# One more attention head keeps its scores in PSUM, and nine thread priorities of a planned emission order move by small steps

## The chip, the cores and the metric

The kernel runs on one core of a Trainium2 chip. The metric is device time in microseconds of one execution, lower is better; the median of several executions is compared. The engines are named as in the profile: PE (TensorE matmuls), PEld (its weight loads), DVE (VectorE), ACT (ScalarE), POOL (GpSimd), and SP, whose queue issues most of the DMAs.

## The reference, cut to what matters

Three layers run in a row, for 4 batches of 576 tokens, 512 wide.

```python
# 1: attention, 8 heads of 64, with a decay per key and a causal mask
scores = scale * q @ k.T + (cum[:, None] - cum[None, :]); scores[causal] = -1e9
attn = softmax(scores); x = concat_heads(attn @ v)
# 2: four attention experts, the best two of four by a gate, causal
for e in range(4):
    q, k, v = x @ wq[e], x @ wk[e], x @ wv[e]
    y += gate[:, e] * (softmax(scale * q @ k.T + mask) @ v @ wo[e])
# 3: low-rank mixing over tokens, then a feed-forward layer of width 2048
u = y + (y.T @ U @ V).T
out = u + relu(u @ w_ch1) @ w_ch2
```

The weights of the third layer come as float64 and are converted in the kernel; products that need it are made as three f16 products of high and low parts.

## The kernel before, in words

Work is written as some hundred Python generators, the threads. A thread yields the name of an engine when it wants to emit instructions on it, or an event, or a buffer ring. The class `Plan` holds a clock of its own for every engine and picks, again and again, the thread with the smallest key. The key is the planned start time in ns plus `PEN` (35.0) times the thread's priority from the table `PR`. So a step of 1 in `PR` is worth 35 ns of planned time; threads whose engine is busy have the same planned start, and then the smaller priority goes first whatever the distance. The order in which steps are picked is the order of the instructions in every engine's queue, and each engine runs its queue in that order.

```python
k = (k + PEN * th["prio"], th["prio"], th["seq"], k)
if best is None or k < best[0]:
    best = (k, th)
```

The heads are taken in the order of `HEADS`, written (layer, batch, head): the eight heads of batch 0 in layer 1, then (1,1,0) and (1,1,1), the four experts (2,0,0) to (2,0,3), the other six heads of batch 1, then experts and heads of the following batches by turns. Counted from 0, (1,1,0) is head 8 and (1,1,1) head 9.

`scores` (L514) makes each head's scores in five row blocks, 64, 192, 320, 448 and 576 keys wide, into PSUM: a ring `sp` of three banks, the widest block in two halves. `softmax` (L542) finds the row minimum of the negated scores with the mask added on DVE, and takes the exponential on ACT into the SBUF tile `sc`. A head counted below `EARLY` does this differently from the others: DVE writes the masked scores back into the same PSUM bank, ACT reads that bank, and the bank is handed back after the exponential; its widest block takes the double bank `acc` (which the feed-forward output uses later) and no `sp` bank. For all other heads DVE writes into `sc`, which has to be free by then, and the `sp` bank is handed back right after DVE.

The exponentials go to `P` as a high part (ACT or DVE) and a low part (mostly POOL). SP then turns them by transposing DMAs into `pt` and `PT`, or, for the first six heads and some experts, PE turns them through its identity matmul (L625). `pair_pv` multiplies by the values, `pv_out` scales into `xn`, splits into `xh` and turns it by DMA into `xt`. `project` (L808) makes queries and keys of layer 2 from `xt`; in batches 1 to 3 it makes its first half, waits for `values_gates` (L845: values and gates, five blocks), and then makes its second half. Both use the two `mm` banks. `prep` (L1045) loads and converts the float64 weights; `fold` (L1014) multiplies the converted tiles `x` by `wtr` into the bank `hid`. `hidden` and `outputs` (L1207, L1240) are the feed-forward layer, in 10 groups of 256 tokens, which PE can take up whenever a group's input `z` is there.

Of the kernel before, what the change touches and what calls it, by code (L numbers as in the profile page):

```python
# [31 lines left out]
XHB = 2  # L32
PBUFS = (1, 1, 1)
VGAT = (2, 1)
EARLY = 8
QUEUE = ('act', 'act', 'sp', 'act')
ACTDMA = 500
PEN = 35.0
# [2 lines left out]
LAG = 800.0  # L41
AHEAD = 5
PROJ_EXP = 15
PR = {'load': 0.5, 'low0': 1.75, 'low': -4, 'zeros': -4, 'scores': 2, 'soft0': 0.75, 'soft2_0': 0.5, 'soft': 3, 'soft2_': 4.75, 'pv0': 2, 'pv': 2, 'pvout0': -4, 'pvout': 3, 'project0': 5, 'project': -4, 'vg0': -1, 'vg': 1.5, 'out0': -2.25, 'out': 9, 'values0': 1.25, 'values': 3, 'wall': 1.75, 'prep': 5, 'f64': -0.25, 'f64_2': 1.25, 'fold': 1.25, 'wf': 2.75, 'w2': 2.5, 'mix': -3.75, 'relu': 2.25, 'store': 0, 'hidden': 4.25, 'outputs': 4.75}
TERMS = ((0, 0), (0, 1), (1, 0))

TURN = {(1, 0): 3, (2, 0): 2, (1, 1): 0, (1, 3): 0}
# [110 lines left out]
class Plan:  # L158
# [21 lines left out]
    def spawn(self, gen, prio=1, t=None):  # L180
        self.seq += 1
        th = {"gen": gen, "t": self.now() if t is None else t, "prio": prio, "seq": self.seq, "last": None}
        self.threads.append(th)
        self.step(th, None)
# [58 lines left out]
def attn_moe_mixer(ctx: ExitStack, tc: tile.TileContext, qk, v, f, wall, wot, wo, w1, w2, u3, v3, out):  # L243
# [208 lines left out]
    def ev(*name):  # L452
        if name not in E_:
            E_[name] = Event(plan)
        return E_[name]
# [58 lines left out]
    def scores():  # L514
        yield ev("mask")
        for key in HEADS:
            yield ev("loaded", key)
            whole, early = key[0] == 1, key in HEADS[:EARLY]

            ops = [(x[:, 0], x.rearrange("d t s -> d (t s)")) for x in HG[key]]  # L520
            for blk in range(KB):
# [4 lines left out]
                for c0, c1 in ([(0, n)] if n <= 512 else [(0, 288), (288, 576)]):  # L526
# [8 lines left out]
                    st.append((sp, c0, c1))  # L535
                spawn(softmax(key, blk, st, early, both), PR[('soft2_' if key[0] == 2 else 'soft') + ('0' if key[1] == 0 else '')])
            if not whole:
# [4 lines left out]
    def softmax(key, blk, st, early, both):  # L542
# [7 lines left out]
        if blk == 0 and on_pe:  # L550
            spawn(turn_head(key), PR['soft0'])
        if first and blk < 2 and not on_pe:
# [56 lines left out]
    def turn_head(key):  # L609

        pt = yield r_pt
        PT[key, True] = pt
        n = Event(plan, 5)
        yield ev("identr")
        for c, blks, k0, k1 in ((0, (0, 1), 0, 5), (3, (2,), 0, 5), (6, (3,), 0, 5), (10, (4,), 0, 4), (14, (4,), 4, 5)):
            for blk in blks:
                yield ev("exp", key, blk)
            r, bank = yield Either(*((r_mm, r_hid) if key[1] == 0 else (r_mm,)))
            flat = bank.rearrange("q a k -> q (a k)") if r is r_hid else bank
            i = 0  # L620
            for blk in blks:
                x = EXP[key, blk]
                yield "pe"
                for kb in range(k0, min(k1, blk + 1)):
                    nc.tensor.transpose(flat[:, 128 * i:128 * i + 128], x[:, 128 * kb:128 * kb + 128], identr)  # L625
                    plan.tensor(110, 128)
                    i += 1
                if k1 > blk:
                    r_sc[blk].free(EXP.pop((key, blk)))

            def out_(r=r, bank=bank, flat=flat, c=c, i=i):
                hi, lo = (pt[:, 15 * t + c:15 * t + c + i, :].rearrange("k c q -> k (c q)") for t in range(2))
                yield from split(hi, lo, flat[:, :128 * i], 2.0 ** 14)
                r.free(bank)
                n.done()
            spawn(out_(), PR['soft0'])
        yield n
        ev("turned", key, 1).done()
# [24 lines left out]
    def pair_pv(kind, b, p):  # L663
# [12 lines left out]
        for j in range(2):  # L676
# [25 lines left out]
            r_pt.free(pt)  # L702
            spawn(pv_out(kind, b, p, j, bank, pv), PR['pvout0' if b == 0 else 'pvout'])
        if not on_pe:
# [7 lines left out]
    def pv_out(kind, b, p, j, bank, pv):  # L712

        h = 2 * p + j
        if kind == 1:
            x = XH[b, p]
        else:
            x = natural(b)[:, p]
        rr = yield r_rr
        yield "dve"  # L720
        if kind == 1:
            ts(rr, pv[:, :, 64], EPS, ALU.add, RV[b][p // 2], ALU.mult)
        else:
            ts(rr, pv[:, :, 64], EPS, ALU.add)
        recip(rr, rr)
        if kind == 2:
            yield ev("gate", b)
            yield "dve"
            tt(rr, rr, GATE[b][:, :, h], ALU.mult)
            if count(E, "gated", b).n == 1:  # L730
                r_wq.free(GATE[b])
            count(E, "gated", b).done()
        xn = yield r_xn
        yield "dve"
        tt(xn, pv[:, :, 0:64], rr[:, :, None].to_broadcast([128, KB, 64]), ALU.mult)
        r_mm.free(bank)
        r_rr.free(rr)
        hi, lo = (x[:, i, :, 64 * j:64 * j + 64] for i in range(2))
        yield from parts(hi, lo, xn)
        r_xn.free(xn)  # L740
        both = count(2, "split", kind, b, p)
        both.done()
        if j == 0:
            return
        yield both
        if p == 0:
            if kind == 1:
                XT[b] = yield r_xt
            else:
                YT[b] = yield r_ynz.of([128, 2, 2, 640], F16, "yt")  # L750
            ev("turn", kind, b).done()
        yield ev("turn", kind, b)
        yield "sp"
        to = (XT if kind == 1 else YT)[b][:, p].rearrange("d t (c q) -> d (t c) q", q=128)
        done = dma(to, x.rearrange("q t c d -> q (t c d)"), transpose=True)
        if kind == 1:
            r_xh.free(x, done.t)
        count(4 if kind == 1 else 2, "out", kind, b).done(done.t)
# [6 lines left out]
    def values(b):  # L765

        es, ss, last = [], [], []
        for half in range(2):
            mx = col(f"mxv{b}{half}", 2)
            vrs = []  # L770
            for i in range(2):
                vr = yield r_vr
                if half == 1 and b == 0:
                    yield ev("rows of first")
                yield QUEUE[3]
                hp = 2 * half + i
                got = dma(vr, v[b][:, :, hp * 128:(hp + 1) * 128], queue(3))
                vrs.append((vr, got))
            for i, (vr, got) in enumerate(vrs):
                yield got  # L780
                junk = yield r_xn.of([128, KB, 128], F16, "junk")
                yield "act"
                abssum(mx[:, i:i + 1], vr, junk)
                r_xn.free(junk)
            e = yield from pow2(f"v{b}{half}", mx, 2)
            es.append(e)
            ss.append(scales(f"v{b}{half}", e, 14)[0])
            if half == 1:
                yield "dve"
                e = col(f"ev{b}")  # L790
                ts(e, es[0], es[1], ALU.max)
                SV[b] = scales(f"v{b}", e, 14)
                RV[b] = [times(f"rv{b}{i}", s, SV[b][1]) for i, s in enumerate(ss)]
                ev("sv", b).done()
            for i, (vr, got) in enumerate(vrs):
                hp = 2 * half + i
                hi = yield r_vp[0]
                lo = yield r_vp[1]
                VP[b, hp] = (hi, lo)
                x = vr.rearrange("p k (h d) -> p k h d", h=2)  # L800
                yield from split(hi[:, :, :, 0:64], lo[:, :, :, 0:64], x, ss[half])
                r_vr.free(vr)
                ev("vp", b, hp).done()
        if b + 1 < B:
            spawn(values(b + 1), PR['values'])


    def project(b):  # L808
# [8 lines left out]
        for p in range(2):  # L817
# [4 lines left out]
            for t in (1, 0):  # L822
                hi, lo = (stg[:, 1], stg[:, 0]) if t else (stg[:, 2], stg[:, 3])
                for c in range(2):
# [8 lines left out]
                    def out_(hi=hi[:, cs], lo=lo[:, cs], pp=pp, n=n):  # L833
                        yield from split(hi, lo, pp[:, :288], float(2.0 ** -PROJ_EXP))
                        r_mm.free(pp)
                        n.done()
                    spawn(out_(), PR['out0' if b == 0 else 'out'])
            ev("project", b, p).done()
# [631 lines left out]
```

## Time and profile before

| | us |
|---|---|
| median of 3 runs (lowest to highest) | 731.06 (730.34 to 732.14) |
| profiled execution, device time | 730.98 |
| its span, first to last instruction | 729.3 |
| PE busy / PEld busy | 652.0 / 450.4 |
| DVE busy / ACT busy / POOL busy | 441.2 / 404.0 / 223.2 |

In the rows further down a line of a timeline reads: start and duration in us, engine, source line (a helper's line, so most have L261, L266, L272 or L284), operation, output<-input, shapes, count, and in square brackets the time that the engine was idle just before it and what ended that. A DMA row of SP gives the time that the issue held the queue. PEclk is the granted share of TensorE's full clock.

### The profile page before, as it was taken

To read this page: it belongs to the slowest core of one execution; us is meant where nothing else is said; L and a number is where in the kernel's file an instruction comes from. 1 tells how busy PE (TensorE), PEld (TensorE's weight loads), DVE (VectorE), ACT (ScalarE), POOL (GpSimd) and SP (SyncE) were. 2 spreads that over 40 slices of the span, in tenths; PEclk is the share of its full clock that TensorE was granted. 3 is DMA by queue.
4 is the path that set the end of the run, shared out by engine and by line. 5 is a ranking of instruction groups with operands and counts; after the bars stand their busy time and mean duration, and the time that the engine had idled before them with its cause. 6 is when DMAs were issued, how large, how long until landed. Compare 5 with 4: busy or idle time off the path is not lost. (4 is left out here: it accounts for less than half of the span.)

```text
span 729.3 us, 15198 instructions
## 1 busy us (share of the span) xinstructions
PE 652.0 (89%) x5622; PEld 450.4 (62%) x5622; DVE 441.2 (60%) x1532; ACT 404.0 (55%) x844; POOL 223.2 (31%) x292
## 2 busy tenths in 40 slices
PE   3777969877678999999998999999999899999997
PEld 2555757756455677577665776676667556665653
DVE  6999887899888746465754376667524653211111
ACT  4757776677778735577765374678623652212121
POOL 4021441101387501355654033465520350000000
PEclk9989999999889999999999999999999999999999
DMA  7735799586567633899877268898842881000000
GB/s 214 197 89 131 168 227 280 148 218 209 122 130 142 96 84 83 173 171 173 158 164 129 64 142 164 142 175 156 160 92 55 140 154 28 30 1 30 1 30 29
DMA packets 206351, 92.94 MB, mean 127 GB/s; under 512 B 178884, under 2 KB 190404, under 8 KB 206244
## 3 DMA queue, kind: packets, MB, share of 16 engines
q1 hardware_dynamic: 195636, 86.59, 55.7%
q10 hardware_dynamic: 10640, 5.38, 2.9%
q8 instruction: 44, 0.72, 0.4%
q14 instruction: 31, 0.25, 0.1%
HBM read 35.68 MB, written 5.16 MB: 56 GB/s over the span
## 5 line engine op out<-in xcount | busy, mean ns | idle before, releaser
L284 POOL TENSOR_TENSOR P<-sc,P 128x192 f16<-128x192 f32 (+4 forms) x186 | 149.3, 816 | 217.2 <-ACT P L266 185.4
L261 PE MATMUL acc<-w2x,g 128*128 128x512 f16 x768 | 180.6, 379 | 2.5 <-DVE nm L272 0.8
L261 PEld LDWEIGHTS <-g 128*128 128x128 f16 x864 | 83.3, 98 | 88.4 <-DVE g L272 2.7
L266 ACT ACTIVATE sc<-sc,nm 128x576 f32<-128x576 f32 (+4 forms) x200 | 108.4, 555 | 37.4 <-DVE nm L272 34.6
L272 DVE SCALAR_TENSOR_TENSOR g<-hid,g 128x512 f16<-128x512 f32 x72 | 49.6, 689 | 119.1 <-ACT g L266 118.9
L261 PE MATMUL hid<-z,wfr 128*128 128x256 f16 x864 | 109.4, 274 | 5.7 <-DVE g L272 2.8
L261 PE MATMUL sp<-Y 128*128 128x192 f32 (+4 forms) x352 | 105.3, 421 | 9.5 <-DVE nm L272 8.3
L266 ACT ACTIVATE g<-hid 128x512 f16<-128x512 f32 x72 | 42.5, 590 | 108.7 <-PE acc L261 47.0
L261 PEld LDWEIGHTS <-wfr 128*128 128x128 f16 x864 | 83.5, 98 | 26.9 <-issue 7.5
L266 ACT ACTIVATE P<-sc 128x576 f16<-128x576 f32 (+4 forms) x183 | 79.9, 460 | 27.4 <-DMA pt<-P 25.0
L261 PEld LDWEIGHTS sp<-Y 128*128 128x128 f32 x352 | 62.0, 202 | 30.2 <-DVE nm L272 15.8
L261 PE MATMUL mm<-V,pt 128*128 128x65 f16 x2046 | 74.0, 194 | 6.3 <-DMA pt<-P 3.8
L261 PEld LDWEIGHTS <-pt 128*128 128x128 f16 x2046 | 69.1, 98 | 10.4 <-DMA pt<-P 4.6
L272 DVE CUSTOM_DVE_ANT_0 sc<-sp,mask 128x192 f32<-128x192 f32 (+4 forms) x120 | 50.8, 426 | 7.3 <-PE sp L261 4.0
L261 PE MATMUL mm<-xt,wall 128*128 128x288 f16 x384 | 50.8, 286 | 3.7 <-DVE stg L272 2.1
L261 PEld LDWEIGHTS <-wall 128*128 128x128 f16 x384 | 37.0, 98 | 16.4 <-issue 4.0
L272 DVE CUSTOM_DVE_ANT_0 sc<-sp,mask,cols 128x288 f32<-128x288 f32 (+4 forms) x80 | 38.6, 489 | 11.1 <-PE sp L261 8.1
L284 POOL TENSOR_TENSOR xh<-xn,xh 128x320 f16<-128x320 f32 x29 | 24.6, 849 | 60.9 <-ACT xh L266 46.0
L261 PE MATMUL hid<-x,wtr 128*128 128x256 f32 x128 | 33.0, 399 | 5.4 <-DVE nm L272 4.4
L284 POOL TENSOR_TENSOR y<-xn,y 128x320 f16<-128x320 f32 x16 | 13.2, 826 | 66.1 <-ACT y L266 61.4
L261 PE MATMUL sp<-Xh 128*128 128x64 f16 (+2 forms) x192 | 29.8, 277 | 1.8 <-DVE nm L272 1.2
L261 PEld LDWEIGHTS hid<-x,wtr 128*128 128x128 f32 x128 | 24.1, 200 | 9.8 <-DVE nm L272 4.3
(142 smaller groups left out, 866.0 us busy)
## 6 DMA issues: line engine op xcount, KB each, us to landing
wd<-in_w SPq DMA_DIRECT2D x32, 512.0 KB
Y<-in_qk SPq DMA_DIRECT2D x32, 288.0 KB
vr<-in_v ACTq DMA_DIRECT2D x16, 320.0 KB
out_dram<-o SPq DMA_DIRECT2D x17, 256.0 KB
Xh<-stg SPq DMA_DIRECT2D x16, 216.0 KB
Xh<-stg SPq DMA_DIRECT2D x16, 144.0 KB
w2x<-in_wall SPq DMA_DIRECT2D x4, 386.0 KB
pt<-P SPq DMA_TRANSPOSE x76
```

What stands on the lines that cost most here:

```text
L261: nc.tensor.matmul(out_, lhsT=lhsT, rhs=rhs, start=start, stop=stop, **kw)
L266: nc.scalar.activation(out_, in_, fn, **kw)
L272: getattr(nc.vector, op)(**kw)
L284: getattr(nc.gpsimd, op)(out=out_, **kw)
```

## The change: what it does

`EARLY` goes from 8 to 9, so head 8 is handled like the eight before it. In `PR` eleven values move. Two of them, `low0` and `low`, are read by no line of the kernel. The nine others: `zeros` (memsets at the start) -4 to -2.5, `pv0` and `pv` 2 to 2.5, `project0` 5 to 6.75, `vg` (values and gates of batches 1 to 3) 1.5 to 3.25, `values0` 1.25 to 1, `wall` 1.75 to 1.5, `prep` 5 to 4.75, `w2` 2.5 to 2.75. No instruction is added or removed apart from head 8's other operands.

```diff
-EARLY = 8
+EARLY = 9
...
-PR = {'load': 0.5, 'low0': 1.75, 'low': -4, 'zeros': -4, 'scores': 2, 'soft0': 0.75, 'soft2_0': 0.5, 'soft': 3, 'soft2_': 4.75, 'pv0': 2, 'pv': 2, 'pvout0': -4, 'pvout': 3, 'project0': 5, 'project': -4, 'vg0': -1, 'vg': 1.5, 'out0': -2.25, 'out': 9, 'values0': 1.25, 'values': 3, 'wall': 1.75, 'prep': 5, 'f64': -0.25, 'f64_2': 1.25, 'fold': 1.25, 'wf': 2.75, 'w2': 2.5, 'mix': -3.75, 'relu': 2.25, 'store': 0, 'hidden': 4.25, 'outputs': 4.75}
+PR = {'load': 0.5, 'low0': 2, 'low': -1.75, 'zeros': -2.5, 'scores': 2, 'soft0': 0.75, 'soft2_0': 0.5, 'soft': 3, 'soft2_': 4.75, 'pv0': 2.5, 'pv': 2.5, 'pvout0': -4, 'pvout': 3, 'project0': 6.75, 'project': -4, 'vg0': -1, 'vg': 3.25, 'out0': -2.25, 'out': 9, 'values0': 1, 'values': 3, 'wall': 1.5, 'prep': 4.75, 'f64': -0.25, 'f64_2': 1.25, 'fold': 1.25, 'wf': 2.75, 'w2': 2.75, 'mix': -3.75, 'relu': 2.25, 'store': 0, 'hidden': 4.25, 'outputs': 4.75}
```

## Rows read from the trace of the kernel before

**Rows 1.** Busy time by stage: us, busy us (instructions) per engine, granted clock, DMA.

```profile
0.00:110.00 110.00, 77.40 (x649) 58.77 (x650) 93.59 (x299) 73.71 (x154) 32.87 (x67) 0.96 0.70 171
110.00:207.00 97.00, 78.50 (x717) 60.15 (x717) 82.69 (x258) 68.37 (x149) 19.18 (x21) 0.94 0.74 192
207.00:225.00 18.00, 13.78 (x109) 9.59 (x109) 17.13 (x55) 14.16 (x28) 14.84 (x14) 0.91 0.52 88
225.00:588.00 363.00, 345.72 (x3237) 240.30 (x3236) 214.91 (x852) 216.27 (x461) 147.22 (x182) 1.00 0.70 136
588.00:729.00 141.00, 136.59 (x919) 81.64 (x915) 32.85 (x70) 31.53 (x56) 9.07 (x11) 1.00 0.14 33
```

**Rows 2.** PE in order of time: head 9's scores to the projection, first feed-forward matmul.

```profile
97.12 0.59 PE L261 MATMUL sp<-Y 128*128 128x192 f32 x2 [1.64 <-DVE nm L272]
97.83 1.99 PE L261 MATMUL hid<-x,wtr 128*128 128x256 f32 x8
99.66 2.42 PE L261 MATMUL sp<-Y 128*128 128x320 f32 x8
102.02 1.45 PE L261 MATMUL mm<-V,pt 128*128 128x65 f16 x42
107.83 3.49 PE L261 MATMUL hid<-x,wtr 128*128 128x256 f32 x8 [4.06 <-DVE nm L272]
111.16 3.10 PE L261 MATMUL mm<-xt,wall 128*128 128x288 f16 x24
...
206.28 0.27 PE L261 MATMUL hid<-z,wfr 128*128 128x256 f16 x1
```

**Rows 3.** DVE in order of time: head 7's 448 block, head 8's, the converted tile.

```profile
81.73 0.63 DVE L272 CUSTOM_DVE_ANT_0 sp<-sp,mask 128x448 f32<-128x448 f32 x1
82.27 0.14 DVE L272 DVE_READ_ACCUMULATOR2_ANT nm<- 128x1 f32 x1
...
93.38 0.61 DVE L272 CUSTOM_DVE_ANT_0 sc<-sp,mask 128x448 f32<-128x448 f32 x1
93.92 0.08 DVE L272 DVE_READ_ACCUMULATOR2_ANT nm<- 128x1 f32 x1
...
107.10 0.67 DVE L272 SCALAR_TENSOR_TENSOR x<-wd,x 128x512 int32<-128x512 int32 x1
```

**Rows 4.** ACT in order of time: head 8's exponential of 448 keys, merged with the next.

```profile
97.68 1.39 ACT L266 ACTIVATE sc<-sc,nm 128x448 f32<-128x448 f32 x2
```

**Rows 5.** Groups by shape: the two forms of the 448 exponential, busy and mean ns.

```profile
L266 ACT ACTIVATE sc<-sc,nm 128x448 f32<-128x448 f32 x40 | 26.3, 658 | 7.8 <-DVE nm L272 7.7
...
L266 ACT ACTIVATE sc<-sp,nm 128x448 f32<-128x448 f32 x8 | 5.1, 632 | 1.1 <-DVE nm L272 1.0
```

**Rows 6.** POOL and SP in order of time, ahead of the projection of batch 0.

```profile
99.25 6.19 SPq L290 DMA_TRANSPOSE pt<-P  x2
105.13 1.13 POOL L284 TENSOR_TENSOR xh<-xn,xh 128x320 f16<-128x320 f32 x1 [2.87 <-ACT xh L266]
105.53 1.20 SPq L290 DMA_TRANSPOSE PT<-P  x1
106.83 1.37 SPq L290 DMA_TRANSPOSE xt<-xh  x1
```

**Rows 7.** Busy time in the hole before that projection, columns as in rows 1.

```profile
104.00:108.00 4.00, 0.17 (x1) 0.17 (x2) 3.74 (x11) 1.81 (x4) 1.13 (x1) 0.94 1.22 215
108.00:112.00 4.00, 4.00 (x15) 3.13 (x16) 2.82 (x4) 3.52 (x9) 2.09 (x3) 0.64 1.01 239
```

**Rows 8.** PE at the start of the projection's second half, batches 1 to 3.

```profile
282.25 1.65 PE L261 MATMUL mm<-xt,wall 128*128 128x288 f16 x12 [0.33 <-DVE lg L272]
427.69 1.64 PE L261 MATMUL mm<-xt,wall 128*128 128x288 f16 x12 [0.61 <-DVE lg L272]
561.54 1.64 PE L261 MATMUL mm<-xt,wall 128*128 128x288 f16 x12 [0.33 <-DVE lg L272]
```

**Rows 9.** PE in order of time: the first matmuls.

```profile
10.77 0.77 PE L261 MATMUL mm<-identr,cols 128*128 128x128 f32 x2 [10.77 <-DVE cols L272]
```

## The prediction

> **What bounds the kernel now.** I read the busy time by stage first, because the average over the span (PE busy 652.0 of 729.3 us) hides two different kernels. Up to 225 us PE is busy 77.40 + 78.50 + 13.78 = 169.7 us, so it stands idle for 55 us, while DVE is busy 93.59 + 82.69 + 17.13 = 193.4 us, 86% of the stage. The granted clock is 0.91 to 0.96 there. From 225 to 588 us PE is busy 345.7 of 363 us at full clock, and after that 136.6 of 141 us [rows 1]. The chain that ended last shows almost only feed-forward matmuls in that last stretch. So the second part is a store of PE work that is worked off at its own speed, and the time is that work plus what PE idles or runs at half clock. The change removes no matmul. It can win or lose in two ways: when the first stage hands over the first input of the feed-forward layer (206.28 us [rows 2]), and in the 17 us of small idle pieces between 225 and 588 us.
>
> Then I read PE, DVE, ACT and SP in order of time around the place where `EARLY` acts, 89 to 111 us. The last things before the projection of batch 0 (111.16 us) are: head 9's scores with a wait of 1.64 us for a bank, a fold, eight more score matmuls of 2.42 us, head 7's value product at about 102 us, an idle hole of 4.06 us, and one fold of 3.49 us [rows 2]. The hole is labelled with DVE's `nm`, but the fold's input `x` is written by the instruction that ends at 107.77 us, 0.06 us before the fold starts [rows 3]; I take that one as what ended it. Behind head 7's value product the chain goes on through POOL (ends at 106.26 us) to the transpose `xt` that SP issues at 106.83 us, just behind the transposes of heads 8 and 9 [rows 6].
>
> **The change part by part.**
>
> *Head 8 in PSUM, its own instructions.* DVE writes its six pieces back to PSUM. Head 7's 448 piece was done so: 0.63 us against 0.61 us for head 8's, and the accumulator read behind it 0.14 against 0.08 us [rows 3]. Six pieces by 0.02 + 0.06 us are 0.5 us more DVE time; I take 0.4, since narrow pieces differ by less. ACT reads PSUM instead of SBUF: 632 against 658 ns [rows 5], five blocks by 26 ns, 0.1 us less. DVE works 3.74 of 4 us just before the projection [rows 7], so nothing hides DVE's part: **+0.4 us**, between 0 and +0.5.
>
> *Head 8 in PSUM, the banks.* A bank now stays taken until the exponential is done. For the 448 block that was from 94.00 us (end of DVE's read) to about 98.4 us, the first of the two merged exponentials at 97.68 us, some 4.4 us longer [rows 3, 4]. In return the widest block uses `acc` and takes two uses off the three `sp` banks. Head 9's pieces then come at other times: its first no longer waits behind two halves of head 8, its later ones wait for exponentials of head 8. The sum of it on PE lies between losing the 1.64 us wait and adding one hold of 4.4 us. What decides is whether it reaches the projection. I expect the later score pieces to slip behind head 7's value product and into the hole, which has 4.06 us free, more than the 2.42 us they take [rows 2]. Two things follow. Head 7's product, and with it `xt`, comes up to 2.42 us sooner, which alone wins nothing, because the fold in front of the projection waits for DVE until 107.77 us. But PE is not idle for 4 us before that fold. The fold took 3.49 us in a stretch with a granted clock of 0.64 (a mix of the levels 1.2 and 2.4 GHz), against 1.99 us for the same eight matmuls at 97.83 us [rows 2, 7]. With the hole filled I take the warm duration: **-1.5 us** for the start of the projection; the bounds are -1.5 - 2.4 = -3.9 us (DVE's tile comes earlier as well) and +4.4 us (a whole hold reaches the path).
>
> The Trainium skill speaks against this part: "PSUM — Partial Sum Buffer", summary of rules for kernel authors, says "Evacuate promptly". By it the sum of this part would be the hold, +4.4 us, where the rows above give -1.5 us; it is the rival of SP's queue below.
>
> *`pv0`, `project0`, `prep`, `values0`, `wall`.* Steps of 0.25 to 1.75 are 9 to 61 ns of planned time, so they only turn round steps that were planned nearly at once. `pv0` falls half a step behind `scores`, with which it was level; in an exact tie scores went first already (they were spawned earlier). `project0` was the last of batch 0's PE threads and stays it. I cost these at nothing, covered by DVE's work in the same stage, and allow one misplaced group either way: 2.42 us [rows 2].
>
> *`vg`.* On PE it falls from before `scores` and `pv` (2 and 2.5) to behind them, still ahead of `hidden` (4.25). The second half of the projection waits for it, and in each of batches 1 to 3 PE idles at its start for a bank, 0.33 + 0.61 + 0.33 = 1.27 us [rows 8]. With scores or value products between, that bank has time to come free: **-1.3 us**. The bounds are -1.3 and, if the second half of the experts starts later and nothing fills PE, one second-half matmul group per batch, 3 x 1.65 = +5 us. I take the near bound, because PE has feed-forward work to put in between.
>
> *`zeros`, `w2`, `low0`, `low`.* The last two are not read. `zeros` moves POOL memsets at the start among others of POOL; PE's first matmul at 10.77 us waits for DVE, not for POOL [rows 9]. POOL works 32.87 of the first 110 us [rows 1]; should a memset come late, its own few tenths would show. `w2` scales weights by 9 ns later. Nothing.
>
> The sum is +0.4 - 1.5 - 1.3 = -2.4 us on the span of 729.3 us. The profiled execution took 730.98 us, 1.7 us outside its span, and the median is 731.06 us, the same within 0.1 us. So the forecast is **731.06 - 2.4 = 728.7 us**. About 0.3%, 2.2 us, is what a measurement of this kernel can tell from no change; the forecast lies at the edge of that.
>
> **The rivals.**
>
> *Nothing arrives.* DVE bounds the first stage (86% busy) and the fold waits for DVE's `x` whatever PE does; small PE waits are only moved, and the bank waits in rows 8 become waits at another place. For it speaks that DVE is busy 3.74 of the 4 us before the projection [rows 7]; against it, that the fold's extra 1.5 us comes after DVE has delivered. Time: 731.06 + 0.4, 731.5 us.
>
> *SP's queue (slower).* SP issues in order, and `xt` stands right behind the transposes of heads 8 and 9: they hold SP from 99.25 to 106.73 us, while POOL had finished `xh` at 106.26 us [rows 6]. There is no slack. If head 8's or 9's `P` comes later because their scores waited for held banks, `xt` waits on SP with them. From the point where the last of these transposes ends after 106.7 us each us reaches the projection, and the whole first stage: with the 4.4 us hold, less the 0.5 us that SP already made it wait, 4 us, 735 us. Against it: two uses less of the `sp` ring.
>
> *A larger gain.* `xt` comes up to 2.4 + 1.6 us sooner, DVE's tile for the fold too, because DVE's steps for head 9 are moved behind it. Then the projection starts about 4 us sooner, and with rows 8 the time is 731.06 - 4 - 1.3, 725.8 us. For it: the row of score pieces ahead of head 7's product; against it: DVE's load.
>
> *Batch 0's chain gets another order after 111 us.* Every pick after the first changed one can come out differently. The stage from 110 to 207 us has 97 - 78.5 = 18.5 us idle on PE [rows 1]; a fifth of it is 3.7 us in either direction, 727.4 or 734.8 us. No row tells its sign.
>
> **How the numbers follow.** The forecast as added up 0.30 (726.5 to 730.5 us); nothing arrives 0.25; SP's queue 0.14; the larger gain 0.12; another order 0.19, with 0.10 on the faster and 0.09 on the slower side. Faster by over 0.3% (under 728.9 us): two thirds of the forecast's case, 0.20, with 0.12 and 0.10: 0.42. Slower by over 0.3%: 0.14 + 0.09 with 0.04 of the case of nothing: 0.27. The rest, 0.31, lies within. The forecast's own range is 726.5 to 730.5 us. The range to 8 in 10 takes in both sides' cases: from 722 us (the larger gain and another order's 3.7 us together) to 736.5 us (SP's queue with another 1.5 us of half clock).
>
> **What would show it.** Right: four matmul records more into `acc` from the query tiles (the widest block of head 8), the hole before the batch-0 projection below 2 us, the fold ahead of it about 2 us long, the projection starting near 109.6 us, the first feed-forward matmul sooner by as much, and the waits of rows 8 gone. Wrong: `xt` issued after 107 us behind transposes of heads 8 or 9, more score waits on PE for `nm` between 89 and 105 us, or a projection that moves without the feed-forward start moving. The prediction fails as a whole if the projection's gain is lost again in the DVE-bound stretch from 140 to 200 us.

## The result, and the profile after

The changed kernel takes 726.34 us (median of 12 runs, 721.79 to 729.88), the kernel before, timed beside it, 731.91 us (12 runs, 730.10 to 734.35). The ratio is 0.9913, 95% interval 0.9889 to 0.9937: 0.87% faster, clear of the 0.3% that the prediction took as the least that can be told from no change. The forecast was 728.7 us, range 722.0 to 736.5.

The profiled execution took 728.6 us with a span of 726.6, so it is one of the longer ones; its span is 2.7 us below that of before, less than the 5.6 us between the medians. Its granted clock over the span was 0.979; of the twelve executions the five at 0.979 or less took 728.0 us in the mean, the seven at 0.983 to 0.988 took 724.9. First the stages of the kernel after, columns as in [rows 1]:

```profile
0.00:225.00 225.00, 169.69 (x1467) 127.70 (x1468) 189.87 (x603) 154.49 (x324) 64.97 (x97) 0.94 0.68 173
225.00:588.00 363.00, 351.89 (x3279) 243.75 (x3277) 226.18 (x867) 218.40 (x465) 155.71 (x192) 1.00 0.69 137
588.00:640.00 52.00, 51.95 (x403) 33.44 (x402) 16.93 (x47) 14.37 (x25) 6.51 (x9) 1.00 0.29 53
```

The first stage is as it was: 169.7 us of PE work by 225 us, 1467 matmul records against 1474. What changed is the middle. PE is busy 351.9 of 363 us there, against 345.7 [rows 1], and does 42 matmul records more. Who PE waited for between 225 and 640 us (total us, times, longest), first before, then after:

```profile
PE mm L261 <- DMA pt<-P: 3.8, 5, 1.5
PE hid L261 <- DVE g L272: 2.8, 4, 1.7
PE mm L261 <- DMA PT<-P: 2.0, 2, 1.4
...
PE mm L261 <- DVE lg L272: 1.3, 3, 0.6
...
PE mm L261 <- DVE stg L272: 0.5, 2, 0.3
```
```profile
PE hid L261 <- DVE g L272: 2.3, 1, 2.3
PE sp L261 <- DVE nm L272: 2.2, 7, 0.4
...
PE mm L261 <- DVE stg L272: 1.3, 3, 0.5
...
PE mm L261 <- DMA pt<-P: 0.6, 1, 0.6
PE mm L261 <- DVE lg L272: 0.3, 1, 0.3
```

The waits of value products for transposes (`pt`, `PT`) were 5.8 us in all and are 0.6. The three waits of [rows 8], `lg`, fell from 1.3 to 0.3, but waits for `stg`, the copy that empties a bank of the projection, came up by 0.8 us. All idle pieces that PE's timeline shows after 225 us sum to 17.9 us before and 11.7 after, 6.2 us less. The busy time of PE over the span is 655.1 against 652.0 us for the same 5622 records, so in this pair of executions some 3 us are given back in slower matmuls; how much of that belongs to the new order and how much to this one execution is not shown.

Where along the span the time is won can be read from the start of the projections of batches 1, 2 and 3 on PE, first before, then after:

```profile
265.46 1.27 PE L261 MATMUL mm<-xt,wall 128*128 128x288 f16 x9
...
409.76 1.27 PE L261 MATMUL mm<-xt,wall 128*128 128x288 f16 x9
...
546.59 6.04 PE L261 MATMUL mm<-xt,wall 128*128 128x288 f16 x48
```
```profile
268.68 6.04 PE L261 MATMUL mm<-xt,wall 128*128 128x288 f16 x48
...
405.35 1.27 PE L261 MATMUL mm<-xt,wall 128*128 128x288 f16 x9
...
543.03 6.04 PE L261 MATMUL mm<-xt,wall 128*128 128x288 f16 x48
```

After is 3.2 us behind at the first and 4.4 us ahead at the second: from batch 1's projection to batch 2's it takes 136.7 us where the kernel before takes 144.3. In the stretches to batch 3's projection and from there to the end it is 0.9 us slower each.

Around the projection of batch 0, PE after, which answers to [rows 2]:

```profile
100.71 1.89 PE L261 MATMUL sp<-Y 128*128 128x448 f32 x6
102.43 0.26 PE L261 MATMUL mm<-V,PT 128*128 128x65 f16 x3
...
108.33 3.60 PE L261 MATMUL hid<-x,wtr 128*128 128x256 f32 x8 [4.05 <-DVE x L272]
111.72 1.39 PE L261 MATMUL mm<-xt,wall 128*128 128x288 f16 x9
115.06 5.14 PE L261 MATMUL mm<-xt,wall 128*128 128x288 f16 x27 [1.94 <-DMA xt<-xh]
...
210.08 0.27 PE L261 MATMUL hid<-z,wfr 128*128 128x256 f16 x1
```

and POOL and SP, which answer to [rows 6]:

```profile
105.78 0.99 POOL L284 TENSOR_TENSOR xh<-xn,xh 128x320 f16<-128x320 f32 x1 [2.16 <-ACT xh L266]
...
100.17 8.51 SPq L290 DMA_TRANSPOSE pt<-P  x2
108.77 1.20 SPq L290 DMA_TRANSPOSE PT<-P  x1
110.07 1.37 SPq L290 DMA_TRANSPOSE xt<-xh  x1
```

The hole of 4 us is still there, the fold behind it is as slow as it was, and the projection has a new wait of 1.94 us: POOL had finished `xh` at 106.77 us, and SP issued its transpose only at 110.07, behind those of heads 8 and 9. The first feed-forward matmul comes at 210.08 us, 3.8 us later than before (this execution was already 1.3 us behind at 76 us, where PE's two orders are still the same). So this pair shows no time won by head 8 in PSUM; the gain lies behind 225 us.

### The profile page after: what moved, and what is told of

It reads as the page before. It is cut to its first block, busy times and chain, and to the rows that moved or that the text cites. A ratio compares the mean times of both kernels' runs of the same rounds, so it can differ in the third digit from the quotient of the medians.

```text
span 726.6 us, 15189 instructions
## 1 busy us (share of the span) xinstructions
PE 655.1 (90%) x5622; PEld 451.5 (62%) x5622; DVE 447.3 (62%) x1536; ACT 402.3 (55%) x838; POOL 227.2 (31%) x296
## 5 line engine op out<-in xcount | busy, mean ns | idle before, releaser
L284 POOL TENSOR_TENSOR P<-sc,P 128x448 f16<-128x448 f32 (+4 forms) x185 | 148.3, 815 | 196.5 <-ACT P L266 173.1
L266 ACT ACTIVATE sc<-sc,nm 64x64 f32<-64x64 f32 (+4 forms) x195 | 105.5, 555 | 43.0 <-DVE nm L272 39.5
L261 PE MATMUL sp<-Y 128*128 128x64 f32 (+3 forms) x348 | 103.0, 417 | 10.4 <-DVE nm L272 8.1
L261 PEld LDWEIGHTS <-wfr 128*128 128x128 f16 x864 | 83.5, 98 | 23.1 <-issue 4.6
L266 ACT ACTIVATE P<-sc 128x448 f16<-128x448 f32 (+4 forms) x180 | 78.1, 458 | 20.4 <-DMA pt<-P 18.1
L261 PEld LDWEIGHTS sp<-Y 128*128 128x128 f32 x348 | 60.9, 199 | 34.4 <-DVE nm L272 17.9
L261 PE MATMUL mm<-V,pt 128*128 128x65 f16 x2046 | 72.5, 194 | 3.9 <-DVE pt L272 1.8
L272 DVE CUSTOM_DVE_ANT_0 sc<-sp,mask 64x64 f32<-64x64 f32 (+4 forms) x115 | 48.9, 426 | 10.3 <-PE sp L261 4.4
L261 PE MATMUL sp<-Xh 128*128 128x64 f16 (+2 forms) x192 | 31.9, 282 | 1.8 <-DVE nm L272 1.8
L261 PE MATMUL mm<-wall,xt 128*128 128x260 f16 (+1 forms) x240 | 30.4, 274 | 1.0 <-DVE lg L272 1.0
```

The lines of the kernel that those rows point to most:

```text
L261: nc.tensor.matmul(out_, lhsT=lhsT, rhs=rhs, start=start, stop=stop, **kw)
L266: nc.scalar.activation(out_, in_, fn, **kw)
L272: getattr(nc.vector, op)(**kw)
L284: getattr(nc.gpsimd, op)(out=out_, **kw)
```

## The experiments

A word on the edits first, from the programs as they are built: with one of the constants changed alone, seven of the twelve (`low`, `low0`, `prep`, `project0`, `pv0`, `values0`, `wall`) leave every engine's instruction order as it was, and `zeros` moves memsets on POOL only. What is left are `EARLY`, `vg`, `w2` and `pv`; a kernel with these four has the changed kernel's order on every engine but for POOL's first memsets. Alone, `EARLY` changes the order from about 89 us on, `w2` from the first relu steps, `vg` from the values and gates of batch 1, `pv` from the last scores of layer 1.

Results, with the ratio to the kernel before on the same chip. "Idle" is the sum of PE's idle pieces after 225 us, "transposes" PE's waits for `pt` and `PT` from 225 to 640 us, "end" PE's busy time of the 52 us from 588 to 640 us; these three are of one profiled execution each. Idle time is part of the time itself, so that column tells where time goes and not why.

| kernel | median us | ratio (95% interval) | idle | transposes | end |
|---|---|---|---|---|---|
| before | 731.91 | 1 | 17.9 | 5.8 | 51.84 |
| after | 726.34 | 0.9913 (0.9889 to 0.9937) | 11.7 | 0.6 | 51.95 |
| only EARLY | 733.20 | 1.0025 (1.0003 to 1.0047) | 17.5 | 4.9 | 51.84 |
| only vg | 749.32 | 1.0252 (1.0213 to 1.0291) | 30.3 | 13.3 | 43.75 |
| only w2 | 729.86 | 0.9970 (0.9944 to 0.9995) | 17.7 | 4.7 | 51.84 |
| only pv | 738.21 | 1.0084 (1.0050 to 1.0117) | 23.1 | 7.8 | 48.26 |
| all but EARLY | 724.96 | 0.9901 (0.9876 to 0.9925) | 13.6 | 3.2 | 51.96 |
| all but vg | 735.38 | 1.0056 (1.0033 to 1.0078) | 19.4 | 4.5 | 48.32 |
| all but w2 | 748.57 | 1.0237 (1.0210 to 1.0265) | 28.7 | 11.9 | 46.21 |
| all but pv | 726.56 | 0.9934 (0.9912 to 0.9956) | 12.6 | 1.8 | 51.95 |
| vg and w2 | 727.29 | 0.9934 (0.9911 to 0.9956) | 12.8 | 2.3 | 51.97 |
| vg, later products | 741.39 | 1.0131 (1.0112 to 1.0150) | 21.5 | 1.4 | 45.47 |
| before, later products | 736.07 | 1.0072 (1.0045 to 1.0098) | 20.5 | 0 | 47.76 |
| after, later products | 734.41 | 1.0036 (1.0015 to 1.0057) | 18.5 | 0 | 45.86 |

The profiled execution of "all but vg" took 730.19 us, 5 us under its median, so its last three columns flatter it.

**One part alone.** Four kernels, each the kernel before with one constant of the change; the diffs show the one entry of `PR` that moves.

```diff
-EARLY = 8
+EARLY = 9
```

> The kernel before with EARLY = 9 alone. The gain of the changed kernel is put down to vg and w2, which act after 210 us, not to head 8. By that theory this kernel is not faster: 0 to +3 us against the kernel before, with the batch-0 projection at 111 to 115 us and the first feed-forward matmul at 206 to 210 us. The rival, that head 8 in PSUM wins the time (as the prediction's 1.5 us), gives -1.5 to -5 us and a first feed-forward matmul sooner than 206 us.

The time is as the first theory had it, slightly slower. Its two marks were missed: the projection of batch 0 started sooner than the 111 us expected, at 108.60 us, and the first feed-forward matmul came at 205.59, just under 206. Head 7's value product is at 100.22:

```profile
98.50 1.88 PE L261 MATMUL sp<-Y 128*128 128x448 f32 x6
100.22 0.26 PE L261 MATMUL mm<-V,PT 128*128 128x65 f16 x3
...
106.13 2.68 PE L261 MATMUL hid<-x,wtr 128*128 128x256 f32 x8 [4.06 <-DVE x L272]
108.60 4.14 PE L261 MATMUL mm<-xt,wall 128*128 128x288 f16 x24
...
205.59 0.27 PE L261 MATMUL hid<-z,wfr 128*128 128x256 f16 x1
```

That is 2.6 us against [rows 2]; 0.95 us of it is the head start that this execution had at 76 us. Of the other 1.6, 0.75 us is head 7's product coming sooner, the fold's input with it, and 0.8 us the fold itself, 2.68 us instead of 3.49. At the first feed-forward matmul 0.7 us are left, less than the head start.

One execution is little, but fourteen kernels of this document were profiled, and PE's order is the same in all up to a value product at about 76 us. Counted from there, the projection starts after 33.1 to 34.2 us in the six kernels with `EARLY` 9 (mean 33.8) and after 33.9 to 34.9 us in the eight with 8 (mean 34.6). So the projection gains some 0.7 us. The hole is 4.05 or 4.06 us in all fourteen. The fold takes 2.68 us only here; elsewhere it takes 3.11 to 3.78. The first feed-forward matmul comes after 128.9 to 132.4 us with 9 and after 129.7 to 132.3 with 8 (means 130.4 and 130.2): what the projection won is gone by then, and the late start in the kernel after is scatter of a size that the kernels with `EARLY` 8 show too.

```diff
-'vg': 1.5
+'vg': 3.25
```

> The kernel before with vg = 3.25 alone. If vg is what wins by letting scores and value products between the five blocks of values and gates, this kernel takes back most of PE's idle pieces from 275 us on: -2 to -5 us, and the wait of the projection's second half for a bank falls below 0.3 us per batch. By the rival, that any new order in that stretch scatters by a few us, it can be anything from -3 to +3 us; by the rival that head 8 or w2 carries the gain it is within 1 us of the kernel before.

Neither the first theory nor scatter by 3 us: 2.5% slower, some 18 us. PE waits for transposes 13.3 us instead of 5.8. In the profiled pair, 20.9 us apart, PE stands idle 12.4 us more after 225 us and is busy 8.2 us more there with the same work. One place where the order costs time, in batch 2: ACT, then SP, then PE, and behind them the same steps of ACT in the kernel before.

```profile
437.83 1.15 ACT L266 ACTIVATE P<-sc 128x576 f16<-128x576 f32 x2 [2.49 <-DMA pt<-P]
438.89 0.30 ACT L266 ACTIVATE lg<-lg,cols 128x20 f32<-128x20 f32 x1
439.09 0.69 ACT L266 ACTIVATE stg<-mm 128x288 f16<-128x288 f32 x2
```
```profile
431.82 2.75 SPq L290 DMA_TRANSPOSE pt<-P  x1
434.66 2.06 SPq L290 DMA_TRANSPOSE PT<-P  x1
```
```profile
441.83 2.74 PE L261 MATMUL mm<-xt,wall 128*128 128x288 f16 x12 [2.13 <-DVE stg L272]
```
```profile
435.42 0.31 ACT L266 ACTIVATE lg<-lg,cols 128x20 f32<-128x20 f32 x1 [0.77 <-DVE lg L272]
435.69 1.15 ACT L266 ACTIVATE P<-sc 128x576 f16<-128x576 f32 x2
436.74 0.39 ACT L266 ACTIVATE stg<-mm 128x288 f16<-128x288 f32 x1
```

With the values and gates later, a softmax write to `P` is ahead of the gate's exponential `lg` in ACT's queue, where the kernel before has it behind. There ACT stands for 2.49 us before this write to the single buffer `P`, whose old content a transpose is still reading. `lg` waits behind it, DVE's gate steps wait for `lg`, DVE's copy `stg` stands behind those, and PE waits for `stg`; the matmuls after that run slowly (2.74 us for the twelve that take 1.63 or 1.64 elsewhere). In the kernel before, the projection's second half ends at 438.2 + 1.6 us in batch 2, here at 446.3 + 1.6. This is one place and not the account of the 18 us: ACT's waits for `P` between 225 and 640 us sum to 25.0 us in the kernel before and to 21.1 with `vg` alone, so there is less of them and not more. By the starts of the projections `vg` alone loses 1.5 us from batch 1 to 2, 9.0 from batch 2 to 3 and 10.8 from there to the end.

```diff
-'w2': 2.5
+'w2': 2.75
```

> The kernel before with w2 = 2.75 alone, which changes the order of weight scaling against relu steps from about 212 us on. The prediction priced it at nothing: -1 to +1 us. If w2 carries the gain it is -3 to -6 us, because relu steps come first and the feed-forward backlog starts sooner.

0.3% faster, interval 0.05 to 0.56%: more than the nothing that the prediction gave it, less than the theory that it carries the gain.

```diff
-'pv': 2
+'pv': 2.5
```

> The kernel before with pv = 2.5 alone; the order differs only from batch 2's end on (about 480 us). Priced at nothing: -1 to +1 us by every theory but that of scatter, by which it can be 2 us to either side.

0.84% slower, outside every expectation. In its trace 3.7 of the 5.2 us of idle that PE has more than before lie between 588 and 640 us, where PE waits mostly for `z`.

The four single effects, taken as ratios, add up to +3.3%. The change that has all four is 0.87% faster. They don't add.

**All parts but one.** Four kernels, each the changed kernel with one constant put back (`EARLY = 8`; `'vg': 1.5`; `'w2': 2.5`; `'pv': 2`).

> The changed kernel with EARLY back at 8. EARLY alone cost 1 to 2 us and its place is the first stage, which does not interact with the others much; so this one should be as fast as the changed kernel or 1 to 3 us faster, 6 to 9 us under the kernel before, with the first feed-forward matmul near 207 us instead of 210. By the rival that all parts interact, it can lose the whole gain: within 3 us of the kernel before or slower.

As expected: without `EARLY` the change is at least as fast (0.9901 against 0.9913, intervals overlap). The first feed-forward matmul came at 208.80 us, not near 207.

> The changed kernel with vg back at 1.5. If the single effects add up, this is the sum of EARLY (+2), w2 (-2) and pv (+6): +6 us against the kernel before. If vg wins in company of w2 although it loses alone, this kernel loses the gain: 0 to +6 us. If vg is bad in any company, it is faster than the changed kernel, 10 us or more under the kernel before.

Without `vg` the gain is gone, 0.56% slower. The single effects would sum to +0.8%, which the errors of three runs don't tell from 0.56%, so this kernel does not decide on adding. `vg`, which alone costs 2.5%, is here worth 1.4%.

> The changed kernel with w2 back at 2.5. If w2 is what turns vg's loss of 18 us into a gain, this kernel is 10 to 25 us slower than the kernel before, with PE idle for transposes and experts' outputs after 590 us as in the run of vg alone. If vg and pv together do it without w2, it stays 3 to 6 us faster than the kernel before.

Without `w2` the kernel is as slow as with `vg` alone. `w2` turns the sign of `vg`.

> The changed kernel with pv back at 2; the order differs only late in the run. By adding, it would be 6 us faster than the changed kernel. By the theory that the small PE waits for transposes decide and fall out differently in every order, it is within 4 us of the changed kernel to either side, and its sum of PE idle pieces after 225 us tells which: less than 12 us if faster, more if slower.

Within the 4 us: the same as the changed kernel by the intervals. Its idle sum is 12.6 us, over the 12 of the expectation and over the changed kernel's 11.7. `pv`, 0.84% alone, does nothing measurable in this company.

**The two that matter, and a test of the waits.** The last four kernels: `vg` and `w2` alone together, and three in which the planner is told that a transposed `P` can be used 1.5 us later, so that value products stand later in PE's queue. That edit changes nothing but the order.

```diff
-            ev("turned", hold, g).done(done.t)
+            ev("turned", hold, g).done(done.t + 1500)
```

> vg = 3.25 and w2 = 2.75 on the kernel before, EARLY 8 and pv 2. If these two together make the change and the other two are bystanders, 5 to 8 us under the kernel before, as the changed kernel, with PE's waits for transposes after 225 us below 3.5 us. If three parts are needed, it lies within 3 us of the kernel before.

Nearly the first theory: 0.66% faster (0.44 to 0.89%), 4.8 us and so just short of the 5 expected, three quarters of the change's 0.87%, and the intervals overlap. PE waits for transposes 2.3 us.

> vg = 3.25 alone, and the planner told that a transposed P is usable 1.5 us later than it thought, so that value products stand later in PE's queue (nothing but the order changes). Theory: what vg alone lost comes from value products that stand in PE's queue ahead of transposes that have not landed (13.3 us of PE waits there, against 5.8 before), so most of the 18 us comes back: 4 us slower to 3 us faster than the kernel before, PE's waits for transposes below 4 us. Rival, the batches' chain is longer with the values and gates late whatever PE waits for: still 10 us or more slower than the kernel before, with small waits on PE.

> The kernel before with the same 1.5 us in the planner and no other edit. Theory: the 5.8 us of PE waits for transposes after 225 us shrink to 1 to 2 us, and the time falls by 2 to 5 us. Rival, value products that stand later only lengthen the chain of each batch: 0 to 5 us slower although the waits shrink.

> The changed kernel with the same 1.5 us in the planner. Its PE waits for transposes are 0.6 us already, so by the theory there is nothing to win: 0 to 4 us slower than the changed kernel. If it gains 3 us or more, the waits are not what these orders differ by, and every new order simply scatters.

In all three the waits for transposes went, to 1.4, 0 and 0 us. In the kernel with `vg` alone that gave back about half of the loss (1.0252 to 1.0131): 9.6 us slower than before (8.2 to 11.0), far from the theory's 4 and at the edge of the rival's 10. In the kernel before and after it cost 0.7% and about 1.2%, the latter some 9 us where 0 to 4 were expected. So my theory, that these waits are what the orders' times differ by, falls; the rival of the second expectation holds. The stretch from 588 to 640 us shows where time went: first before (after has 51.95 us busy there, see above), then after with later products.

```profile
588.00:640.00 52.00, 51.84 (x422) 33.02 (x419) 18.54 (x49) 15.91 (x30) 9.07 (x11) 1.00 0.30 57
```
```profile
588.00:640.00 52.00, 45.86 (x342) 28.89 (x340) 16.84 (x53) 16.48 (x32) 8.91 (x12) 0.90 0.26 55
```

and who PE waited for there, after with later products:

```profile
PE hid L261 <- ACT z L266: 2.5, 1, 2.5
PE mm L261 <- DVE cols L272: 1.3, 1, 1.3
PE hid L261 <- DVE z L272: 1.1, 1, 1.1
PE mm L261 <- DVE th L272: 0.9, 1, 0.9
```

PE has run out of feed-forward work before the last batch's `z` exists, stands for 6.1 us, mostly behind the chain of the mixing step, and the granted clock of the stretch is 0.90. Before that stretch, from 225 to 588 us, PE's idle sum is 11.6 against 10.9 us in the kernel after: no less, although no wait for a transpose is left. In the pair without the change it is 15.5 against 17.1 us, with 4.2 us at the end against none.

## Why the prediction was right or wrong

The direction and the range came out right, and so did one of the two places that the prediction named, the small idle pieces of PE after 225 us. The other did not: the first input of the feed-forward layer is handed over no sooner. The sum was -2.4 us, measured were -5.6 (0.63 to 1.11%). That the number fell into the range is in good part luck: the largest term, -1.5 us for head 8's banks, belongs to a part that alone makes the kernel slower, and the gain hangs on `vg` together with `w2`, which was priced at nothing. Of the signs named beforehand, the four records into `acc` came and the waits of [rows 8] shrank but did not go; the hole, the fold, the projection and the feed-forward start did not come as said, and `xt` was issued after 107 us, a sign of being wrong. The terms:

- *Head 8's own instructions, +0.4 us.* Borne out: its six pieces and the reads behind them take 3.43 us on DVE after and 3.14 before, 0.29 us more, most of it in the reads. The reads behind the pieces of 320, 448 and twice 288 keys take 0.14 us, but those behind the pieces of 64 and 192 keys 0.08, as for heads that write to SBUF. Head 8's pieces of 192 and 448 keys, then head 9's of 448:

```profile
90.89 0.37 DVE L272 CUSTOM_DVE_ANT_0 sp<-sp,mask 128x192 f32<-128x192 f32 x1
91.28 0.08 DVE L272 DVE_READ_ACCUMULATOR2_ANT nm<- 128x1 f32 x1
...
96.15 0.62 DVE L272 CUSTOM_DVE_ANT_0 sp<-sp,mask 128x448 f32<-128x448 f32 x1
96.69 0.14 DVE L272 DVE_READ_ACCUMULATOR2_ANT nm<- 128x1 f32 x1
...
101.77 0.62 DVE L272 CUSTOM_DVE_ANT_0 sc<-sp,mask 128x448 f32<-128x448 f32 x1 [0.28 <-PE sp L261]
102.32 0.08 DVE L272 DVE_READ_ACCUMULATOR2_ANT nm<- 128x1 f32 x1
```

- *Head 8's banks, -1.5 us.* This step failed. The late score pieces did not slip behind head 7's value product, the hole stayed 4.05 us, and so the fold stayed slow. The projection came some 0.7 us sooner, because head 7's product and the fold's input did, and that was lost again before the feed-forward start, the case that the prediction's last sentence calls its failure as a whole. The measured price of this part alone is +0.25% (0.03 to 0.47%). The rival of SP's queue was the right mechanism to fear: `xt` was issued 3.3 us after POOL had finished in the kernel after and 2.3 us with `EARLY` alone (106.88 against 104.56 us), against 0.6 in [rows 6]; over all profiled kernels it is 1.8 to 3.3 us with `EARLY` 9 and 0.4 to 1.6 with 8. In the kernel after the projection waits 1.94 us for it behind its first nine matmuls; its start was not held back. The hold itself was overestimated: the 448 block was held until the end of the exponential below, 98.29 us, 1.5 us and not 4.4 after DVE's read at 96.69 + 0.14.

```profile
97.67 0.62 ACT L266 ACTIVATE sc<-sp,nm 128x448 f32<-128x448 f32 x1
```

"Evacuate promptly", the rule of the Trainium skill ("PSUM — Partial Sum Buffer", summary), points to the side that was measured, though +4.4 us, one hold, is more than twice the 1.8 us found.

- *`vg`, -1.3 us.* The waits named fell by 1.0 us, and half of that or more came back as `stg`. But the term was mis-sized, and its bounds were wrong: alone `vg` costs 2.5%, more than three times the upper bound of +5 us; beside `w2` it is worth 1.4%, of which the waits for `lg` are the least part. What I had left out is that a thread moved on PE moves the order of ACT, DVE and SP too, where one wait holds what stands behind it, as in the example of batch 2; how much of the 18 us such waits make is not shown.

- *`w2`, nothing, and `pv`, which has no term at all.* Failed: `w2` alone is -0.3% and decides the sign of `vg`; `pv` alone is +0.84%. "9 ns of planned time" is no bound, because one changed pick can alter all later ones: `w2` alone changes every engine's order from about 211 us to the end. The allowance of one misplaced group, 2.42 us, was too small for the same reason.

- *`project0`, `pv0`, `prep`, `values0`, `wall`, `low`, `low0`, nothing.* Right, and more than cover: alone they change no order. `zeros` alone moves POOL's memsets only.

Which constants make the gain is shown: `vg` and `w2` together make about three quarters of it or more, and leaving either out loses it. Where it is won can be read, too: in the four kernels that have both, with the planner as it is, batch 1's projection to batch 2's takes 136.7 to 139.2 us, against 144.3 before, 145.8 with `vg` alone and 143.1 with `w2` alone, and from there to the end 1.7 to 2.5 us more than before. How it is made up in the profiled pair: 6.2 us less PE idle after 225 us, of it 5.2 in waits for transposes, and 3 us given back in slower matmuls. That less waiting for transposes causes the gain is not shown; the later products speak against it as a rule. In the table the time goes with the idle sum, from 11.7 us to 30.3, and the kernels that are slower by 0.36% or more all have PE short of work in the end stretch (43.75 to 48.32 of 52 us busy), the others not. Why `w2`, whose scaling steps are over at 252 us in the kernel before, turns the sign of a change that acts from batch 1 on was not tried in parts and stays open.

## What to carry to other kernels

In a planned order, a constant that breaks near ties is a switch into another order and not a small step: test it alone and left out, and don't add single effects, for here +3.3% by addition was -0.87% in fact. Find first which constants change any engine's order at all; of these twelve, seven did not. When PE lives on a backlog, look at the end stretch as well: in the slower orders here PE ran out of work there.

## What the runs showed of the hardware that was not expected

The accumulator read on DVE took 0.08 us behind every reduction that writes to SBUF in the kernel before (0.076 to 0.086 us, 240 reads). Behind reductions that write to PSUM it took 0.13 to 0.14 us in 33 of 48 cases and 0.08 us in the other 15, among them all eight of 64 keys; what decides is open. A pair of transposing DMAs of `P` took 6.19, 7.54 and 8.51 us of SP's time in three executions at the same place (before, `EARLY` alone, after), a wait of 0.9 to 1.4 us between the two included; the second DMA alone took 3.5, 4.4 and 5.4 us. Of the 3.2 us by which the next transpose was issued later after than before, 2.3 come from this pair.
